# RWKV-7 attention and a dense mixture of experts on one core: chunks of 64 tokens for two batches at a time, with the triangular inverse by substitution on GpSimd

## The chip, the core and the metric

One NeuronCore of a Trainium2 chip. Its engines run side by side, each through its own instructions in order: TensorE (PE; its weight loads are listed apart as PEld) multiplies matrices into PSUM, VectorE (DVE) and ScalarE (ACT) read and write SBUF and PSUM, GpSimd (POOL) works on SBUF, and SyncE (SP) issues DMA transfers. The metric is the device time of one execution in microseconds (us); lower is better. Everything is fp32.

## What is computed

An attention block over 4 batches, 8 heads, 768 tokens and 40 dimensions per head carries a state of 40x40 per head from token to token; its output, with the heads put side by side (3072 tokens x 320), goes through four experts whose outputs are mixed by normalised probabilities.

```python
for t in range(S):                                   # S = 768
    y[:, :, t] = np.einsum('bhd,bhde->bhe', rt, state)
    Sa = np.einsum('bhde,bhe->bhd', state, at)
    state_decay = state * wt[:, :, None, :] - np.einsum('bhd,bhe->bhde', Sa, bt)
    state = state_decay + np.einsum('bhd,bhe->bhde', vt, kt)
...
x = np.ascontiguousarray(attn_out.transpose(0, 2, 1, 3)).reshape(B * S, H * D)
p = domain_probs / (domain_probs.sum(-1, keepdims=True) + 1e-09)
for e in range(E):                                   # E = 4, w1: 320 x 1024, w2: 1024 x 320
    h = np.maximum(x @ w1[e], 0.0)
    out += p[:, e:e + 1] * (h @ w2[e])
```

Both kernels compute the recurrence in chunks: within a chunk, products over pairs of tokens replace the loop, and the rows Sa solve a triangular system (I - F) Sa = A S^T + E V, where F is strictly lower triangular within the chunk.

## The kernel before

A unit is one batch and 128 tokens, which are four chunks of 32; there are 24 units. The 8 heads stand in 4 pairs, one head of each at partitions 0-39 and the other at 64-103; s is that half.

`within(u)` prepares what needs no state. It transposes the inputs so that a head's dimensions are on partitions (`turn`), scans the decays to their running products G (L217) and takes reciprocals (L222), scales A, K and N, and transposes some of them back (`turn_back`). `products` (L204) makes the token-by-token matrices E, C and F; a masked copy keeps the part inside each 32-token chunk. Then comes the inverse of I - F by levels (L264-L281): from blocks of 1 to blocks of 2, 4, 8, 16 and 32, each of four rounds taking a transpose `pq`, a product `pfq` and a product `pqfq` for each half, all of 128x128, with a copy between them. At the end `pu` applies the inverse.

`step(q, c)` runs four times per unit, a chunk each: `psa` gives that chunk's rows of Sa from the state, `psn` turns the state for the outputs, `psd` and two operations of VectorE renew the state. `outputs` makes y (`px`, `py`), scales it and sends it by 8 DMAs, one per head, into xT, the mixture's input, whose rows are the 320 features in groups of 120, 120 and 80.

`mixture` takes 256 tokens (two batches' units): for each expert, products `ph` of all three row groups with 256 columns (L376), a relu by ScalarE (L381), products `po` with 320 columns (L387), and a scaled sum by VectorE (L395). It is a generator; `mix()` runs one of its pieces after each chunk's step and inside the inverse's rounds.

The order of each engine's instructions follows the order of the code, but for a scheduler that may exchange neighbours whose waits would end at other times; on the chip each engine keeps the order that it was given. All names of one PSUM pool share buffers: `big` has three, `small` two, `ph` two and `po` one. SyncE's queue has the loads of the next unit, the writes to xT and the outputs; ScalarE's queue has the weights' loads at the start.

Of the kernel before, what the change touches and what calls it, by code (L numbers as in the profile page):

```python
# [15 lines left out]
def kernel(  # L16
# [34 lines left out]
    L = 32  # L51
    NCK = P // L
    NT = S // P
    NJ = H // 2
    SL = (0, 64)
    NF = F // P
    HG = 3
    NG = -(-H // HG)
    ROWS = [min(HG, H - g * HG) * D for g in range(NG)]
    NTOK = B * S  # L60
    NH2 = 2 * P
    LEVELS = [2 ** i for i in range(L.bit_length() - 1)]

    const = ctx.enter_context(tc.tile_pool(name="const", bufs=1))
    wts = ctx.enter_context(tc.tile_pool(name="wts", bufs=1))
    sb = ctx.enter_context(tc.tile_pool(name="sb", bufs=2))
    mo = ctx.enter_context(tc.tile_pool(name="mo", bufs=2))
    ps = ctx.enter_context(tc.tile_pool(name="ps", bufs=1, space=bass.MemoryType.PSUM))

    def big(name):  # L70
        return ps.tile([P, 512], FP32, name=name, tag="big", bufs=3)

    def small(name, shape):
        return ps.tile(shape, FP32, name=name, tag="small", bufs=2)

    # Constants.
# [7 lines left out]
    def mask(name, half):  # L84
        """1 at [s, t] with s in the left and t in the right half of one block of 2 * half."""
        blk = 2 * half
        f = sb.tile([P, P], FP32, name=name + "_f", tag="Q", bufs=2)
        m = const.tile([P, P], I32, name=name)
        fv = f[:].rearrange("p (n i) -> p n i", i=blk)
        nc.vector.memset(f[:], 1.0)  # L90
        nc.gpsimd.affine_select(
            out=fv, in_=fv, pattern=[[-blk, P // blk], [0, blk]], compare_op=ALU.is_ge, fill=0.0,
            base=0, channel_multiplier=1,
        )
        nc.gpsimd.affine_select(
            out=fv, in_=fv, pattern=[[blk, P // blk], [0, blk]], compare_op=ALU.is_ge, fill=0.0,
            base=half - 1, channel_multiplier=-1,
        )
        nc.vector.memset(fv[:, :, 0:half], 0.0)
        nc.vector.tensor_copy(out=m[:], in_=f[:])  # L100
        return m

    mask_level = [mask(f"mask{h}", h) for h in LEVELS]
    mask_chunk = const.tile([P, P], I32, name="mask_chunk")
    nc.vector.tensor_tensor(out=mask_chunk[:], in0=mask_level[0][:], in1=mask_level[1][:], op=ALU.add)
    for m in mask_level[2:]:
        nc.vector.tensor_tensor(out=mask_chunk[:], in0=mask_chunk[:], in1=m[:], op=ALU.add)
# [309 lines left out]
    while pieces:  # L417
        mix()
# [28 lines left out]
```

## Time and profile before

| what | value |
|---|---|
| time, median of 3 runs | 2876.21 us (2873.59 to 2889.38) |
| profiled execution, first to last instruction | 2906.9 us (its time is recorded as this span alone) |
| TensorE matrix products | 19360 instructions |
| VectorE, ScalarE, GpSimd busy | 753.7, 497.8, 44.2 us |
| mean granted TensorE clock | 0.824 of full speed |
| data moved by DMA | 44.75 MB |

How to read the rows below. The page gives, for each engine, busy time, its share of the span and the number of instructions; a row of digits gives the clock that TensorE was granted in 40 slices of the span, in tenths. The chain of work that ended last goes back from the last instruction to what released it. A group row reads: line, engine, operation, out<-in, shape, count | busy us, mean ns of one | idle time before, and what ended it. A row of the chain in order of time reads: start, us, what. A row of the timeline reads: start, us, engine, line, operation, with merged instructions counted behind an x. A row of the table by windows has the stretch and its length, then busy us and instructions for PE, PEld, DVE, ACT and POOL, then the clock, the share of the DMA engines and GB/s. A mean duration of a TensorE instruction contains its overlap with its neighbours, so the pace is read from rows in which many follow each other.

### The profile page before, as it was taken

The page shows a single profiled execution, that of the slowest core. Times are in us where ns is not written, and L with a number is a line of the kernel's source. Part 1 is how long each engine was busy: PE and PEld are TensorE (multiplying, and loading weights), DVE is VectorE, ACT ScalarE, POOL GpSimd, SP SyncE. Part 2 cuts the span into 40 slices and gives each one's busy share as a digit, 9 for nine tenths or more (in the row PEclk, how much of TensorE's full clock was granted, in tenths as well). Part 3 has the DMA queues.
Part 4 walks back from the last instruction along what each step waited for, and adds up shares of the span by engine and source line. Part 5 has one row for each costly group of instructions (what it writes and reads, how often), then busy time and mean ns, then how long its engine had stood idle before and what let it go on. Part 6 is the DMA issues. An engine that isn't in the chain of part 4 may idle for free.

```text
span 2906.9 us, 43054 instructions
## 1 busy us (share of the span) xinstructions
PE 2781.9 (96%) x19360; PEld 2235.6 (77%) x19360; DVE 753.7 (26%) x1400; ACT 497.8 (17%) x985; POOL 44.2 (2%) x88
## 2 busy tenths in 40 slices
PE   1989999999999999999999999999999999999999
PEld 1778787786887877778778788787777878878867
DVE  2232322123122232222222322222122222322310
ACT  0121121121211211212112121121211212202201
POOL 2000000000000000000000000000000000000000
PEclk9776988887878877968779797796787879969969
DMA  8001001001010010000101101001010010010000
GB/s 172 4 14 17 11 7 21 3 14 22 1 17 13 10 17 6 17 9 9 21 1 16 22 1 17 10 12 17 1 21 5 12 21 3 15 21 1 3 7 5
DMA packets 171710, 44.75 MB, mean 15 GB/s; under 512 B 155400, under 2 KB 170248, under 8 KB 171528
## 3 DMA queue, kind: packets, MB, share of 16 engines
q1 hardware_dynamic: 162816, 31.48, 6.5%
q10 hardware_dynamic: 8712, 10.54, 1.5%
q8 instruction: 152, 2.49, 0.4%
q14 instruction: 30, 0.25, 0.0%
HBM read 34.13 MB, written 3.93 MB: 13 GB/s over the span
## 4 chain that ended last, share of the span: by engine, by line
PE 95%; DMA 2%; DVE 1%; SPq 1%; POOL 0%; issue 0%; ACT 0%; ACTq 0%; DVEq 0%
PE ph L376 21%; PE po L387 19%; PE psd L328 7%; PE pfq L204 6%; PE pqfq L204 6%; PE pq L271 4%; PE psn L316 4%; PE py L352 3%; PE py L348 3%; PE psa L309 3%; PE pf L204 2%; PE pev L250 2%; PE py L349 2%; PE px L204 2%; PE pe L204 2%; PE pc L204 2%
## 5 line engine op out<-in xcount | busy, mean ns | idle before, releaser
L376 PE MATMUL ph<-xT,w_sb 120*128 120x256 f32 (+1 forms) x2304 | 672.8, 431 | 38.8 <-DMA xT<-Y 38.8
L387 PE MATMUL po<-w_sb,hs 128*128 128x320 f32 x1536 | 579.8, 520 | 1.3 <-DVE osb L395 0.6
L376 PEld LDWEIGHTS ph<-xT,w_sb 120*128 120x128 f32 (+1 forms) x2304 | 459.5, 215 | 104.7 <-DMA xT<-Y 21.9
L387 PEld LDWEIGHTS po<-w_sb,hs 128*128 128x128 f32 x1536 | 314.1, 221 | 112.2 <-issue 27.0
L280 DVE COPY_PREDICATED QT<-mask,pqfq 128x512 f32<-128x512 int32 x192 | 140.5, 732 | 560.2 <-PE pqfq L204 560.2
L273 ACT COPY Q<-pq 128x512 f32<-128x512 f32 x192 | 112.5, 586 | 541.7 <-PE pq L271 541.7
L204 PEld LDWEIGHTS pfq<-Q,FT 128*128 128x128 f32 x1536 | 193.6, 199 | 8.1
L204 PE MATMUL pfq<-Q,FT 128*128 128x128 f32 x1536 | 195.9, 282 | 0.0
L328 PEld LDWEIGHTS psd<-natV,KN 32*40 32x40 f32 x1472 | 144.4, 146 | 64.6 <-DVE state L334 42.8
L204 PEld LDWEIGHTS pqfq<-QT,FQ 128*128 128x128 f32 x1536 | 185.2, 191 | 6.6
L381 ACT ACTIVATE hs<-ph 128x512 f32<-128x512 f32 x192 | 114.6, 597 | 432.5 <-PE ph L376 432.5
L204 PE MATMUL pqfq<-QT,FQ 128*128 128x128 f32 x1536 | 188.2, 276 | 0.0
L328 PE MATMUL psd<-natV,KN 32*40 32x40 f32 x1472 | 177.7, 238 | 2.5 <-DVE state L333 2.5
L328 PE MATMUL psd<-Sa,KN 32*40 32x40 f32 x1472 | 176.9, 236 | 0.0
L333 DVE TENSOR_TENSOR state<-psd,state 40x160 f32<-40x160 f32 x184 | 59.3, 322 | 380.5 <-PE psd L328 380.5
L319 ACT COPY SN<-psn 40x160 f32<-40x160 f32 x192 | 54.6, 285 | 590.6 <-PE psn L316 589.1
L328 PEld LDWEIGHTS psd<-Sa,KN 32*40 32x40 f32 x1472 | 148.6, 150 | 2.6
L271 PE MATMUL pq<-ident,QT 128*128 128x128 f32 x768 | 143.1, 316 | 2.5 <-DVE QT L280 1.5
L277 ACT COPY FQ<-pfq 128x512 f32<-128x512 f32 x192 | 112.3, 585 | 151.4 <-PE pfq L204 151.4
L309 PEld LDWEIGHTS psa<-state,AT 40*32 40x32 f32 x1536 | 77.4, 131 | 76.8 <-issue 62.6
L316 PEld LDWEIGHTS psn<-ident,state 40*40 40x40 f32 x1536 | 91.1, 141 | 54.5 <-issue 25.8
L271 PEld LDWEIGHTS pq<-ident,QT 128*128 128x128 f32 x768 | 99.2, 160 | 38.3 <-DVE QT L280 16.4
(103 smaller groups left out, 2527.9 us busy)
## 6 DMA issues: line engine op xcount, KB each, us to landing
w_sb<-in_moe_w_dram ACTq DMA_DIRECT2D x4, 1280.0 KB
w_sb<-in_moe_w_dram ACTq DMA_DIRECT2D x8, 480.0 KB
natR<-in_r_dram SPq DMA_DIRECT2D x24, 160.0 KB
natK<-in_k_dram SPq DMA_DIRECT2D x24, 160.0 KB
natV<-in_v_dram SPq DMA_DIRECT2D x24, 160.0 KB
natW<-in_w_dram SPq DMA_DIRECT2D x24, 160.0 KB
natB<-in_b_dram SPq DMA_DIRECT2D x24, 160.0 KB
natA<-in_a_dram SPq DMA_DIRECT2D x24, 160.0 KB
```

What stands on the lines that cost most here:

```text
L204: nc.tensor.matmul(out=p[:, j * P:(j + 1) * P], lhsT=lhsT[:, j, :], rhs=rhs[:, j, :], start=True, stop=True)
L271: nc.tensor.transpose(out=p[:, j * P:(j + 1) * P], in_=q.QT[s][:, j, :], identity=ident[:])
L273: nc.scalar.copy(out=Q[s][:].rearrange("p j t -> p (j t)"), in_=p[:])
L277: nc.scalar.copy(out=FQ[s][:], in_=products("pfq", FT(2 * u + s), Q[s]))
L280: nc.vector.copy_predicated(out=q.QT[s][:], mask=over_heads(m), data=products("pqfq", FQ[s], q.QT[s]),)
L309: nc.tensor.matmul(out=pa[ck, j, :], lhsT=q.AT[rows(s), j, ck], rhs=st[rows(s), j, :], start=True, stop=True,)
L316: nc.tensor.matmul(out=pn[rows(s), j, :], lhsT=st[rows(s), j, :], rhs=ident[rows(s), rows(s)], start=True, stop=True,)
L328: nc.tensor.matmul(out=pd[rows(s), j, :], lhsT=q.KN[ck, i, h, 0:D], rhs=x[ck, h, 0:D], start=(i == 0), stop=(i == 1),)
L348: nc.tensor.matmul(out=o, lhsT=q.KN[:, 0, h, :], rhs=q.CT[s][:, j, :], start=True, stop=False)
L376: nc.tensor.matmul(out=ph[:, i, :], lhsT=w1_sb[0:ROWS[g], e, g, f * P:(f + 1) * P], rhs=xT[0:ROWS[g], g, :], start=(g == 0), stop=(g == NG ...
L381: nc.scalar.activation(out=hs[:], in_=ph[:], func=ACTF.Relu)
L387: nc.tensor.matmul(out=po[:], lhsT=Hs[f][:, s * P:(s + 1) * P], rhs=w2_sb[:, e, f, :], start=(f == 0), stop=(f == NF - 1),)
```

## The change

The whole attention part is rewritten, and the mixture is cut into smaller pieces.

- A unit is now one chunk of 64 tokens of two batches, the first batch's tokens on partitions 0-63 and the second's on 64-127. There are 24 units as before, and one `step` per unit in place of four. Units are prepared two ahead: the loop runs `step(u)` and `within(u + 2)`.
- The inverse: F's 32x32 diagonal blocks of all heads (4 token groups x 8 heads) are gathered by masked copies into one tile Fd, transposed in 32x32 blocks by VectorE into X, and inverted by column substitution on GpSimd, two instructions for each of 30 columns. VectorE transposes the result into QTc and Qc. One round on TensorE (`pY`, `pQ`, 32x32 products) adds the block beside the diagonal of each 64-token chunk.
- Products over 64 partitions (`products`, `psd`, and the last 64 of the 320 rows of the first weight) go in the order half 0, half 1, half 0, half 1. Products into 64 PSUM partitions (`from_tokens`) alternate the half of the output.
- Scaling is done with tokens on partitions (`pg` turns G back), which saves the transposes back. C K is finished in `within` and added by GpSimd at the end (YC).
- xT's row groups are 128, 128 and 64, the last one kept twice, on both halves. A unit writes 11 DMAs to xT.
- The mixture yields 32 pieces of 256 tokens; the loop takes 16 of them per unit, spread over the 15 places where `step` and `within` yield. PSUM has four `big` buffers and four shared by `ph` and `po`.

The core of the diff, the new side, as the old functions are printed above:

```diff
+    def products(name, lhsT, rhs):
+        p = [big(f"{name}{s}") for s in range(2)]
+        for j in range(NJ):
+            for s in range(2):
+                nc.tensor.matmul(
+                    out=p[s][:, j * P:(j + 1) * P], lhsT=lhsT[half(s), j, :], rhs=rhs[half(s), j, :],
+                    start=True, stop=True,
+                )
+        return [pairs(x[:]) for x in p]
+
+    def from_tokens(name, x, m):
+        p = big(name)
+        for j in range(NJ):
+            for s in range(2):
+                h = 2 * j + s
+                nc.tensor.matmul(
+                    out=p[half(s), j * P:(j + 1) * P], lhsT=x[:, h, :], rhs=m[:, h, :], start=True, stop=True,
+                )
+        return p
...
+        pf = products("pf", q.AT, NT)
+        F10 = sb.tile([P, H, Q], FP32, name="F10")
+        for s in range(2):
+            for i in range(P // Q):
+                o = quarter(i)
+                nc.vector.copy_predicated(
+                    out=fd[o, :, NJ * s:NJ * s + NJ].rearrange("p c j -> p j c"),
+                    mask=mask_low[o, None, :].to_broadcast([Q, NJ, Q]), data=pf[s][o, :, o],
+                )
+            for i in (1, 3):
+                nc.scalar.copy(out=of_slot(F10[quarter(i)], s), in_=pf[s][quarter(i), :, quarter(i - 1)])
+        X = sb.tile([P, Q, Q], FP32, name="X", tag="q", bufs=3)
+        tmp = sb.tile([P, Q * Q // 4], FP32, name="tmp")
+        nc.vector.transpose(out=X[:].rearrange("p c r -> p (c r)"), in_=fd[:].rearrange("p c h -> p (c h)"))
+        for j in range(1, Q - 1):
+            m = Q - 1 - j
+            t = tmp[:, 0:j * m].rearrange("p (c r) -> p c r", c=j)
+            nc.gpsimd.tensor_tensor(
+                out=t, in0=X[:, j:j + 1, j + 1:Q].to_broadcast([P, j, m]),
+                in1=X[:, 0:j, j:j + 1].to_broadcast([P, j, m]), op=ALU.mult,
+            )
+            nc.gpsimd.tensor_tensor(out=X[:, 0:j, j + 1:Q], in0=X[:, 0:j, j + 1:Q], in1=t, op=ALU.add)
+        yield 1
+        KT = turned("KT", q.K)
+        pc = products("pc", VT, q.RT)
+        CT = causal(pc)
+        yield 1
+        pyc = from_tokens("pyc", q.K, CT)
...
+        pe_ = products("pe", KT, q.AT)
+        ET = causal(pe_)
+        yield 1
+        pev = from_tokens("pev", q.V, ET)
...
+        nc.vector.transpose(out=QTc[:].rearrange("p h r -> p r h"), in_=X[:].rearrange("p c r -> p r c"))
+        nc.vector.transpose(out=Qc[:].rearrange("p h c -> p c h"), in_=X[:])
...
+        py = big("pY")
+        for h in range(H):
+            hh = (h % 2) * NJ + h // 2
+            for i in (1, 3):
+                nc.tensor.matmul(
+                    out=py[quarter(i - 1), hh * Q:(hh + 1) * Q], lhsT=F10[quarter(i), h, :],
+                    rhs=QTc[quarter(i), hh, :], start=True, stop=True,
+                )
...
+            for f in range(4):
+                for g in range(2):
+                    nc.tensor.matmul(
+                        out=ph[f % 2][:, f // 2, :], lhsT=w1_sb[:, e, g, (f0 + f) * P:(f0 + f + 1) * P],
+                        rhs=xT[:, g, :], start=(g == 0), stop=False,
+                    )
+                if f % 2:
+                    for i in range(2):
+                        nc.tensor.matmul(
+                            out=ph[i][:, f // 2, :], lhsT=w1_last[i * DT:(i + 1) * DT, e, (f0 + f) // 2, :],
+                            rhs=xT[i * DT:(i + 1) * DT, 2, :], start=False, stop=True,
+                        )
+                    yield 1
...
+    drive(within(units[0]), 0, 1)
+    load(1)
+    drive(within(units[1]), 0, 1)
+    for u in range(NU):
+        q = units[u]
+        if q.bp == 0:
+            xT = sb.tile([P, 3, NTOK], FP32, name="xT", tag="xT", bufs=2)
+        gens = [step(q, xT)]
+        if u + 2 < NU:
+            load(u + 2)
+            gens.append(within(units[u + 2]))
+        drive(chain(*gens), PIECES // 2, 14)
+        if q.bp == B // 2 - 1:
+            work.append(mixture(q.c, xT))
```

The new `step` makes, in this order, `prh` (A times the state; VectorE adds EV), `psn` (the state turned), `prt`, `psa` (the inverse applied), `pst`, `px`, `psd` with the state's renewal, and `py`; between each two of them is a place for a piece of the mixture.

TensorE before, in the middle of the program, where the inverse of a unit begins: `pev` and `pf` end the preparation, then the first round's `pq`, `pfq`, `pqfq` for both halves, with the mixture's `ph` between.

```order
L204 MATMUL pf<-A,N 128x128 x2
L271 MATMUL pq<-ident,QT 128x128 x4
L376 MATMUL ph<-xT,w_sb 128x256 x3
L271 MATMUL pq<-ident,QT 128x128 x4
L376 MATMUL ph<-xT,w_sb 128x256 x2
L204 MATMUL pfq<-Q,FT_134 128x128 x4
L204 MATMUL pfq<-Q,FT_136 128x128 x4
L376 MATMUL ph<-xT,w_sb 128x256 x5
L204 MATMUL pqfq<-QT,FQ 128x128 x8
```

TensorE now, at the end of a unit's preparation in the middle of the program: `pe`, one piece of `ph`, `pev`, nine `po`, then `pY`, which reads QTc, and `pQ`, which reads what ScalarE copied of `pY`.

```order
L216 MATMUL pe_1758<-AT,KT 128x128
L458 MATMUL ph<-xT,w_sb 128x256 x4
L464 MATMUL ph<-xT,w_last 128x256 x2
L228 MATMUL pev<-TT_112,natV_96 64x128 x8
L477 MATMUL po<-w_sb,hs 128x320 x9
L336 MATMUL pY<-QTc,F_1633 32x32 x16
L477 MATMUL po<-w_sb,hs 128x320
L347 MATMUL pQ<-Yq,Qc 32x32
L477 MATMUL po<-w_sb,hs 128x320
L347 MATMUL pQ<-Yq,Qc 32x32 x15
L477 MATMUL po<-w_sb,hs 128x320 x5
```

The twelve products of `pq`, `pfq` and `pqfq` per half and pair are gone, and 16 + 16 small products stand in their place, behind the nine `po`.

GpSimd now, at the end of one unit's substitution and the start of the next one's, with the semaphores that an instruction waits for (Pool is its own engine's; before, this engine had two copies of a constant per unit there):

```order
L296 TENSOR_TENSOR tmp<-X 128x58 [waits Pool_49]
L300 TENSOR_TENSOR X<-X,tmp 128x29x2 [waits Pool_49]
L296 TENSOR_TENSOR tmp<-X 128x30 [waits Pool_49]
L300 TENSOR_TENSOR X<-X,tmp 128x30 [waits Pool_49]
L331 COPY QT_116<-QTc 32x8x32 [waits DVE_49]
L434 TENSOR_TENSOR Y<-Y,YC 128x512 [waits DVE_49,Pool_49]
L296 TENSOR_TENSOR tmp<-X 128x30 [waits DVE_49]
L300 TENSOR_TENSOR X<-X,tmp 128x30 [waits Pool_49]
L296 TENSOR_TENSOR tmp<-X 128x58 [waits Pool_49]
```

And VectorE around the end of the substitution, in the same unit as TensorE's rows above:

```order
L236 COPY_PREDICATED TT_112<-mask_up,pe_1758 128x4x128 [waits PE_49]
L319 STREAM_TRANSPOSE QTc<-X 128x32x32 [waits DVE_49,Pool_49]
L320 STREAM_TRANSPOSE Qc<-X 128x32x32
L487 SCALAR_TENSOR_TENSOR osb<-po,gate,osb 128x320 [waits PE_49] x2
L374 TENSOR_TENSOR RH<-prh,EV 128x512 [waits PE_49]
```

The two transposes wait for GpSimd's last addition; the scaled additions of `po` and the addition to `prh` stand behind them.

More of the change, by code (lines that the diff above doesn't have):

```diff
@@ L220, in within @@
         )
[L221 to L225 removed]
+        q.gl = sb.tile([P, 2 * NJ, 1], FP32, name="gl", tag="gl", bufs=2)
@@ L403 @@
[L403 to L418 removed]
+        nc.vector.tensor_tensor(out=q.K[:, :, 0:D], in0=n["K"][:], in1=gp[:], op=ALU.mult)
@@ new lines, with mix, drive, chain @@
+    PIECES = E * (2 * 2 + 2 * 2)
+    work = []
+    def mix():
+        while work:
+            if next(work[0], None) is not None:
+                return True
+            work.pop(0)
+        return False
+    def drive(gen, n_pieces, n_yields):
+        done = 0
+        for i, _ in enumerate(gen):
+            while done * n_yields < (i + 1) * n_pieces and mix():
+                done += 1
+    def chain(*gens):
+        for g in gens:
+            yield from g
+    drive(within(units[0]), 0, 1)
```

560 lines of the change are left out of this document (286 added, 274 removed).

## The prediction

> **What bounds the kernel now.** I read the page's busy times first, then its chain of work that ended last, the row of the granted clock, and one stretch of the table by windows that leaves out the start and the end.
>
> ```profile
> PE 2781.9 (96%) x19360; PEld 2235.6 (77%) x19360; DVE 753.7 (26%) x1400; ACT 497.8 (17%) x985; POOL 44.2 (2%) x88
> PE 95%; DMA 2%; DVE 1%; SPq 1%; POOL 0%; issue 0%; ACT 0%; ACTq 0%; DVEq 0%
> PEclk9776988887878877968779797796787879969969
> 200.00:2800.00 2600.00, 2554.05 (x17957) 2046.56 (x17955) 686.79 (x1282) 456.91 (x910) 25.75 (x42) 0.82 0.07 12
> ```
>
> TensorE is busy for 2554 of the 2600 us from 200 to 2800 and carries 95% of the chain. GpSimd does nothing there, and the DMA engines are 7% busy. So the time is TensorE's work divided by its clock, whose mean is 0.82 of full speed. The change must be priced in TensorE time and in waits that would put TensorE idle, where it now almost never is.
>
> How fast TensorE goes, shape by shape, I take from rows of the chain of waits at full clock. They tell when one group took over from another, without the overlap of its neighbours:
>
> ```profile
> 303.07 1.79 PE pfq L204 x16
> 312.52 0.44 PE pat L188 x4
> 317.79 0.73 PE psd L328 x16
> 836.31 3.47 PE ph L376 x16
> 2836.93 4.31 PE po L387 x16
> ```
>
> A 128-column instruction costs 0.11 us, a transpose of 128 columns as much, a small one 0.046, `ph` with 256 columns 0.217 and `po` with 320 columns 0.269. Each fp32 product is two such instructions and each transpose one: 768 `pfq` products stand in the page's groups as x1536, 96 `pw` transposes as x96.
>
> **The change, part by part.** Both programs have 24 units of the same 128 rows, so I price one unit and multiply.
>
> Removed first: the inverse by levels, four times per unit.
>
> ```profile
> L204 PE MATMUL pfq<-Q,FT 128*128 128x128 f32 x1536 | 195.9, 282 | 0.0
> L204 PE MATMUL pqfq<-QT,FQ 128*128 128x128 f32 x1536 | 188.2, 276 | 0.0
> L271 PE MATMUL pq<-ident,QT 128*128 128x128 f32 x768 | 143.1, 316 | 2.5 <-DVE QT L280 1.5
> ```
>
> That is 527 us of TensorE time. The four state steps per unit (`psd`, `psa`, `psn`, small products) become one step over 64 tokens of two batches.
>
> New products alternate between partitions 0-63 and 64-127. The old kernel does this once by accident, where the scheduler interleaved `pf` (partitions 0-39) with `pe` (partitions 64-103). This is the timeline of TensorE there:
>
> ```profile
> 605.85 0.82 PE L204 MATMUL pf<-A,N 40*128 40x128 f32 x5
> 606.40 0.37 PE L204 MATMUL pe<-A,K 40*128 40x128 f32 x1
> 606.51 0.27 PE L204 MATMUL pf<-A,N 40*128 40x128 f32 x1
> 606.61 0.27 PE L204 MATMUL pe<-A,K 40*128 40x128 f32 x1
> 606.62 0.27 PE L204 MATMUL pf<-A,N 40*128 40x128 f32 x1
> 606.73 0.27 PE L204 MATMUL pe<-A,K 40*128 40x128 f32 x1
> 606.73 0.27 PE L204 MATMUL pf<-A,N 40*128 40x128 f32 x1
> ```
>
> Two start together, a hundredth of a microsecond or less apart, and the next pair 0.11 us later: such a pair costs one. The price of changing the tile's shape also shows, where `py` alternates 64-column products with 40x40 ones:
>
> ```profile
> 702.37 0.36 PE py L348 x2
> 702.73 0.22 PE py L349 x2
> 702.95 0.42 PE py L352 x8
> ```
>
> The two `py` of L348 that follow the 40x40 group take 0.36, the two behind them 0.22: 0.14 per change, and I use 0.13.
>
> TensorE's work in one new unit at full clock:
> - 44 transposes at 0.11: 4.8 us.
> - 48 products over 64 partitions (`pf`, `pc`, `pe`, `px`, `psd`), in pairs: 96 instructions, 48 slots of 0.11: 5.3.
> - 32 products into 64 PSUM partitions (`pyc`, `pev`, `psa`, `py`): 64 instructions at 0.11: 7.0. No row shows two column halves side by side; it lies between 3.5 (paired) and 11.5 (0.18, as the 0.36 above).
> - 32 products of 64 columns (`prh` and the state's part of `py`): 64 at half of 0.11: 3.5.
> - 32 products of 32x32 (`pY`, `pQ`): 64 at 0.046: 2.9.
> - By the order, 38 changes of tile shape at 0.13: 4.9.
> - The mixture, half of its 256 tokens' work: 64 `ph` at 0.217 make 13.9, the last 64 rows of the first weight in pairs 16 x 0.217 = 3.5, 64 `po` at 0.269 make 17.2: 34.6, in 16 pieces of 2.16.
>
> Sum 63.0 us per unit, 1512 for 24, where TensorE was busy for 2782 us at clock 0.82.
>
> (The Trainium skill, TensorE: Matmul & The Clock Gate, Part 3 on packing small matmuls, says that outputs in separate column groups run side by side too, with 2.38x for three. By it the third item would be 3.5, and the total some 40 us lower; no row here shows it.)
>
> **The new wait.** The inverse of the 32-blocks now runs on GpSimd: 60 instructions in a row, each waiting for the one before, with 30 to 240 elements a partition, 9920 in sum. `pY` on TensorE waits for the end of it, and TensorE is in order. GpSimd's rows of before:
>
> ```profile
> L260 POOL COPY QT<-ident 128x512 f32<-128x512 f32 x48 | 29.4, 614 | 2615.2 <-PE pu L289 2615.2
> L91 POOL TENSOR_SCALAR_AFFINE_SELECT mask_f<-mask_f 128x128 f32<-128x128 f32 x5 | 2.3, 461 | 0.5 <-DVE mask_f L90 0.5
> L79 POOL TENSOR_SCALAR_AFFINE_SELECT ident<-ident 128x128 f32<-128x128 f32 x1 | 0.3, 292 | 0.0
> L433 POOL MEMSET const-float32-0.0<- 128x1 f32 x1 | 0.1, 98 | 0.3 <-issue 0.3
> 1.62 1.20 POOL L91 TENSOR_SCALAR_AFFINE_SELECT mask_f<-mask_f 128x128 f32<-128x128 f32 x2
> ```
>
> Fixed cost 0.098 us; a copy costs (614-98)/512 = 1.0 ns an element. No instruction with two inputs stands in the trace. Lower end: the copy's rate, 9.9 + 60 x 0.098 = 16 us. Upper end: the first masks, in runs of 2 and 4 elements, took about 0.6 us for 128 elements, so 4.7 ns each and 47 us in all. I take twice the copy, because two inputs must be read: 19.8 + 5.9, and for short runs (0.6 - 0.292)/64 = 4.8 ns for each of the 930 runs, 4.5. That is 30 us.
>
> (The Trainium skill, GPSIMD Engine Reference, section 3.1, gives 4497 ns for a two-input add of 2048 elements, 2.2 ns each, and calls this engine the wrong one for elementwise work. By it the elements take 22 us and the same sum 32; the trace has no such row.)
>
> Around it stand VectorE's pieces, from these rows:
>
> ```profile
> L333 DVE TENSOR_TENSOR state<-psd,state 40x160 f32<-40x160 f32 x184 | 59.3, 322 | 380.5 <-PE psd L328 380.5
> L217 DVE TENSOR_TENSOR_SCAN G<-w_shift,first 128x528 f32<-128x528 f32 x24 | 30.2, 1257 | 25.6 <-ACT w_shift L215 25.6
> L247 DVE COPY_PREDICATED ET<-mask_chunk,pe 128x512 f32<-128x512 int32 x48 | 34.6, 721 | 111.8 <-PE pe L204 111.8
> L222 DVE RECIPROCAL GI<-G 128x512 f32<-128x512 f32 x24 | 80.2, 3343 | 0.1
> ```
>
> Eight masked copies of 128 elements at 0.3 (nearest, the 160-element row) make 2.4; two block transposes of 1024 elements, between the masked copy's and the scan's 1.4 and 2.4 ns an element less their fixed part, I put at 1.2 each; 0.2 for the hand-overs. From the end of `pf` to `pY`: 2.4 + 1.2 + 30 + 1.2 + 0.2 = **35 us**, 21 to 52 by the ends.
>
> What covers it: in the order, 5.25 mixture pieces (11.3), `pKT`, `pc`, `pyc`, `pe`, `pev` (5.7) and 13 changes of shape (1.7), 18.7 us at full clock, about 21.5 at 0.87. So TensorE idles some 13 us per unit, and nothing overtakes `pY`. On VectorE the two block transposes wait at the head for the same end; behind them stand two scaled additions of `po` and the addition of `prh`, which TensorE needs only behind `pY`. On GpSimd the copies into QT and the addition of YC follow; they are used a stage later.
>
> From `pY` to the next `pf` TensorE has 63.0 - 18.7 = 44.3 us of work. I take clock 0.87 there (0.82 before; dense pieces stand between all stages now, but a long idle time comes first): 51 us, with 2 us for hand-overs that one piece of 2.16 us doesn't cover (the reciprocal of 320 elements, 3343 x 320/512 = 2.1, is the longest): **53**. A unit's turn is 35 + 53 = 88 us.
>
> The loads become 12 DMAs of half the size per unit and the writes to xT 11 in place of 8, on a queue whose engines are 7% busy; each has a unit's turn to land. I cost them at nothing; without that cover it would be some microseconds a unit.
>
> Start and end:
>
> ```profile
> 51.94 1.12 PE L188 MATMUL pb<-ident,natB 128*128 128x128 f32 x4 [17.27 <-ACT w_shift L215]
> 2820.00:2907.00 87.00, 81.06 (x320) 62.53 (x320) 4.41 (x8) 9.55 (x16) 0.00 (x0) 0.94 0.02 6
> ```
>
> The weights hold ScalarE's queue until about 52 us, as before. Then come four units' preparations without a mixture, their chains wholly bare: 44 + 46 + 2 x 58 (with a step of 12) = 206, so 258. Twenty turns of 88 make 1760. Two last steps take 30 each, and 50 pieces at 2.16 and full clock 108, with the output 170. Sum 258 + 1760 + 170 = 2188 us against the span of 2906.9. The median of the runs is 2876.21, 0.9894 of that span, so 2165 us.
>
> **The rivals.**
> - *The substitution is hidden*: GpSimd goes at the copy's rate, 16 us. The chain is 21 us, as long as its cover, and TensorE stays the bound: 63/0.87 + 3 = 75 per turn, start 202: 202 + 1508 + 170 = 1880, or 1860 us. For it speaks that GpSimd's rows are all short; against it, that each instruction reads two operands and waits for the last.
> - *The clock stays down behind the idle time*: with 0.7 between `pY` and `pf` the turn is 35 + 66 = 101 and the sum 258 + 2020 + 180 = 2458, or 2432 us. The clock row shows 0.7 in many slices of a TensorE that never idles.
> - *The substitution takes the bound, and the kernel is slower*: the sum is 1348 + 24 x chain, equal to 2907 at a chain of 65 us, GpSimd at 1.0 us an instruction. At 1.3 us (78 us, chain 83) it is 3340, or 3305 us. The first masks' 0.6 us for 128 elements is the dearest row; this needs twice that, so I give it little.
>
> **How the numbers follow.** Forecast 0.58, hidden 0.23, low clock 0.13, slower 0.05, and 0.01 for a balance near nothing. The likeliest gives 2165 us, on its own 2030 to 2300. The range takes in the hidden case and the low clock: 1820 to 2430. Faster by over 0.5% (about what a measurement of this kernel can tell from no change) has 0.94, the same 0.01, slower 0.05.
>
> **What would show it.** GpSimd's `tmp` and `X` groups, 60 per unit, near 0.5 us each; `pY` first in TensorE's waits, released through VectorE's `QTc` by GpSimd, near 13 us a unit; TensorE's busy share near 80%; paired starts in `pf`, `px`, `psd` and the `w_last` products; clock 0.8 to 0.9. A GpSimd mean under 0.3 or over 0.9 us makes the chain wrong; no idle time at `pY` with a time over 2000 makes TensorE's own sum wrong.

## The result, and the profile after

| | before | after |
|---|---|---|
| median of the runs side by side | 2882.15 us (2873.59 to 2889.38, 4 runs) | 2210.34 us (2209.20 to 2211.01, 4 runs) |
| ratio | | 0.7666 (95%: 0.7642 to 0.7690) |
| profiled span | 2906.9 us | 2209.1 us |
| mean granted TensorE clock | 0.824 | 0.833 |

The forecast was 2165 us with a range of 1820 to 2430. From the page of the changed kernel: busy times, the row of the clock, the chain that ended last, the groups that matter, and then two rows of the waits of TensorE and VectorE (engine and line, what was waited for: us in all, times, longest).

```profile
PE 1522.0 (69%) x11592; PEld 1115.2 (50%) x11592; DVE 636.7 (29%) x930; ACT 318.3 (14%) x667; POOL 803.4 (36%) x1596
...
PEclk9656777977978979879788798797797887978999
...
PE 48%; POOL 34%; DVE 11%; issue 5%; DMA 1%; ACT 0%; SPq 0%; ACTq 0%; DVEq 0%; POOLq 0%
...
L296 POOL TENSOR_TENSOR tmp<-X 128x30 f32<-128x30 f32 (+4 forms) x720 | 348.1, 483 | 545.4 <-DVE X L292 490.9
...
L300 POOL TENSOR_TENSOR X<-X,tmp 128x30 f32<-128x30 f32 (+4 forms) x720 | 369.6, 513 | 56.4
...
L319 DVE STREAM_TRANSPOSE QTc<-X 128x1024 f32<-128x1024 f32 x24 | 47.6, 1983 | 686.4 <-POOL X L300 686.4
L283 DVE COPY_PREDICATED Fd<-mask_low,pf 32x128 f32<-32x128 int32 x192 | 139.0, 724 | 115.1 <-PE pf L216 112.4
```

```profile
PE pY L336 <- DVE QTc L319: 577.3, 24, 31.1
DVE QTc L319 <- POOL X L300: 686.4, 24, 30.2
```

TensorE is no longer the bound: it is busy for 69% of the span, and GpSimd and VectorE carry 45% of the chain that ended last. Most of TensorE's idle time sits in one wait. Of 687 us (2209.1 - 1522.0) it stood 577.3 at `pY`, 24 us a unit, for VectorE's transposition QTc, and VectorE stood there for GpSimd's last addition to X. This is one such unit, in the timeline of TensorE (start, us, what, and in brackets the idle time ahead):

```profile
1024.12 1.06 PE L216 MATMUL pf<-NT,AT 64*128 64x128 f32 x16
...
1039.58 5.11 PE L477 MATMUL po<-w_sb,hs 128*128 128x320 f32 x18
1069.23 1.07 PE L336 MATMUL pY<-QTc,F 32*32 32x32 f32 x32 [24.54 <-DVE QTc L319]
...
1079.82 1.20 PE L369 MATMUL prh<-AT,state 128*64 128x64 f32 x32
1080.94 1.09 PE L205 MATMUL psn<-ident,state 128*128 128x128 f32 x8
...
1089.83 1.09 PE L228 MATMUL psa<-QT,RHt 128*64 128x128 f32 x16
1090.86 1.99 PE L458 MATMUL ph<-xT,w_sb 128*128 128x256 f32 x8
...
1101.78 0.44 PE L420 MATMUL py<-TT,n_tok 128*64 128x128 f32 x4
...
1103.73 2.42 PE L477 MATMUL po<-w_sb,hs 128*128 128x320 f32 x8
```

In the same unit on VectorE, and GpSimd's first two and last of the 60 instructions:

```profile
1025.21 5.91 DVE L283 COPY_PREDICATED Fd<-mask_low,pf 32x128 f32<-32x128 int32 x8 [3.57 <-PE pf L216]
1031.22 1.25 DVE L292 STREAM_TRANSPOSE X<-Fd 128x1024 f32<-128x1024 f32 x1
...
1067.11 1.97 DVE L319 STREAM_TRANSPOSE QTc<-X 128x1024 f32<-128x1024 f32 x1 [29.67 <-POOL X L300]
```

```profile
1032.54 0.24 POOL L296 TENSOR_TENSOR tmp<-X 128x30 f32<-128x30 f32 x1 [19.90 <-DVE X L292]
1032.86 0.24 POOL L300 TENSOR_TENSOR X<-X,tmp 128x30 f32<-128x30 f32 x1
...
1066.81 0.27 POOL L300 TENSOR_TENSOR X<-X,tmp 128x30 f32<-128x30 f32 x1
```

`pf` ends at 1025.18 and `pY` starts at 1069.23: a chain of 44.0 us from one to the other, and it takes 44.0 to 44.6 us in the other units too. Of it 5.9 are the masked copies, 1.25 and 1.97 the two transpositions, and 34.6 GpSimd. Its instructions are busy for 29.9 us a unit, (348.1 + 369.6)/24; the rest is 0.08 us between each two that depend on each other, as between 1032.54 + 0.24 and 1032.86.

### The profile page after: what moved, and what is told of

Its sections match the earlier page's. It is cut to its first block, busy times and chain, and to the rows that moved or that the text cites. A ratio compares the mean times of both kernels' runs of the same rounds, so it can differ in the third digit from the quotient of the medians.

```text
span 2209.1 us, 28307 instructions
## 1 busy us (share of the span) xinstructions
PE 1522.0 (69%) x11592; PEld 1115.2 (50%) x11592; DVE 636.7 (29%) x930; ACT 318.3 (14%) x667; POOL 803.4 (36%) x1596
## 4 chain that ended last, share of the span: by engine, by line
PE 48%; POOL 34%; DVE 11%; issue 5%; DMA 1%; ACT 0%; SPq 0%; ACTq 0%; DVEq 0%; POOLq 0%
POOL X L300 17%; POOL tmp L296 16%; PE po L477 16%; PE ph L458 11%; DVE Fd L283 6%; PE ph L464 4%; DVE QTc L319 2%; PE psd L402 2%; PE prh L369 1%; PE psn L205 1%; DVE X L292 1%; PE px L216 1%; PE pf L216 1%; PE pQ L347 1%; PE psa L228 1%
## 5 line engine op out<-in xcount | busy, mean ns | idle before, releaser
L296 POOL TENSOR_TENSOR tmp<-X 128x30 f32<-128x30 f32 (+4 forms) x720 | 348.1, 483 | 545.4 <-DVE X L292 490.9
L477 PE MATMUL po<-w_sb,hs 128*128 128x320 f32 x1536 | 489.6, 468 | 0.0
L336 PE MATMUL pY<-QTc,F 32*32 32x32 f32 x768 | 25.5, 236 | 577.3 <-DVE QTc L319 577.3
L458 PE MATMUL ph<-xT,w_sb 128*128 128x256 f32 x1536 | 390.6, 395 | 2.9 <-DMA xT<-Y 2.9
L300 POOL TENSOR_TENSOR X<-X,tmp 128x30 f32<-128x30 f32 (+4 forms) x720 | 369.6, 513 | 56.4
L458 PEld LDWEIGHTS ph<-xT,w_sb 128*128 128x128 f32 x1536 | 277.6, 192 | 69.1 <-issue 29.3
L319 DVE STREAM_TRANSPOSE QTc<-X 128x1024 f32<-128x1024 f32 x24 | 47.6, 1983 | 686.4 <-POOL X L300 686.4
L283 DVE COPY_PREDICATED Fd<-mask_low,pf 32x128 f32<-32x128 int32 x192 | 139.0, 724 | 115.1 <-PE pf L216 112.4
L464 PE MATMUL ph<-xT,w_last 64*128 64x256 f32 x768 | 148.2, 436 | 0.0
L464 PEld LDWEIGHTS ph<-xT,w_last 64*128 64x128 f32 x768 | 63.2, 188 | 69.1 <-issue 67.7
L259 DVE RECIPROCAL gp<-gp 128x320 f32<-128x320 f32 x24 | 51.4, 2143 | 0.0
```

Source lines behind the costliest of these rows:

```text
L259: nc.vector.reciprocal(out=gp[:], in_=gp[:])
L283: nc.vector.copy_predicated(out=fd[o, :, NJ * s:NJ * s + NJ].rearrange("p c j -> p j c"), mask=mask_low[o, None, :].to_broadcast([Q, NJ, Q ...
L296: nc.gpsimd.tensor_tensor(out=t, in0=X[:, j:j + 1, j + 1:Q].to_broadcast([P, j, m]), in1=X[:, 0:j, j:j + 1].to_broadcast([P, j, m]), op=AL ...
L300: nc.gpsimd.tensor_tensor(out=X[:, 0:j, j + 1:Q], in0=X[:, 0:j, j + 1:Q], in1=t, op=ALU.add)
L319: nc.vector.transpose(out=QTc[:].rearrange("p h r -> p r h"), in_=X[:].rearrange("p c r -> p r c"))
L336: nc.tensor.matmul(out=py[quarter(i - 1), hh * Q:(hh + 1) * Q], lhsT=F10[quarter(i), h, :], rhs=QTc[quarter(i), hh, :], start=True, stop=True,
```

## The experiments

**Is the chain the bound, or does the idle time bring the clock down?** Two kernels shorten the substitution, the first to every second column, the second to none. Their inverses are therefore not the right ones; each ran once.

```diff
-        for j in range(1, Q - 1):
+        for j in range(1, Q - 1, 2):       # e1_half
+        for j in range(0):                 # e2_none
```

> Every second column of the substitution is left out (30 GpSimd instructions per unit in place of 60), so the inverse is not the reference's. Chain theory (pf to pY, 44 us, stands on the path of all 24 units, and TensorE idles 21 to 25 us at its end): the chain is cut by some 17 us, less than the idle time, so all of it counts: 2210 - 24 x 17 = about 1800 us, idle time at pY about 6 us a unit. Rival (the clock gives it back: TensorE without idle time is granted 0.82 as in the old kernel): a turn of 63/0.82 + 3 = 80 us, about 2010 us. Second rival (something else of the turn is nearly as late, VectorE's or ScalarE's part): 2100 us or more.

> The substitution is left out whole (no GpSimd instruction between X and QTc), so the inverse is not the reference's. Chain theory: the cut of 34.6 us is more than the idle time of 23 us, so the time falls to TensorE's own work, a turn of 65 us: 2210 - 24 x 23 = about 1660 us, no idle time at pY, and the second half of the substitution is worth only 6 x 24 = 140 us more than the first half's 410. Rival (clock): about 2010 us as with half of it.

Measured: 1855.6 us with half, 1622.3 us without. The waits at `pY` with half, and the row of the clock without:

```profile
PE pY L336 <- DVE QTc L319: 271.3, 24, 13.8
```

```profile
PEclk9677999999999999999999999999999999999999
```

The chain falls from 44.0 to 26.8 us, the wait from 577 to 271, and without the substitution there is none. The clock goes up as the idle time goes, from 0.833 to 0.907 and 0.947. So the wait is the bound and the clock follows it, not the other way round. With half, the time is 55 us above the 1800 expected. The wait fell by 12.8 us a unit where the chain fell by 17.2, because the order of TensorE changed with the edit: in the middle of the program one to three pieces of the mixture fewer stand between `pf` and `pY`.

**Is it GpSimd's pace?** The same substitution runs on VectorE, in one run.

```diff
-            nc.gpsimd.tensor_tensor(
+            nc.vector.tensor_tensor(
                 out=t, in0=X[:, j:j + 1, j + 1:Q].to_broadcast([P, j, m]),
...
-            nc.gpsimd.tensor_tensor(out=X[:, 0:j, j + 1:Q], in0=X[:, 0:j, j + 1:Q], in1=t, op=ALU.add)
+            nc.vector.tensor_tensor(out=X[:, 0:j, j + 1:Q], in0=X[:, 0:j, j + 1:Q], in1=t, op=ALU.add)
```

> The 60 instructions of the substitution run on VectorE in place of GpSimd; the result is the same. Chain theory: an instruction of 160 elements takes VectorE 0.32 us, so 60 take 19 to 23 us in place of 34.6, with some 3 us of other VectorE work between them: the chain is 10 us shorter, about 1970 us. Rival (VectorE's queue becomes the late one: the masks and the state's renewal stand behind the substitution): 2100 us or more, with TensorE waiting at px, pyc or prh.

Measured: 1777.8 us, far below both. Its group row and its waits:

```profile
L300 DVE TENSOR_TENSOR X<-X,tmp 128x30 f32<-128x30 f32 (+4 forms) x720 | 237.8, 330 | 22.6
```

```profile
PE pY L336 <- DVE QTc L319: 108.9, 24, 21.9
```

An instruction takes 330 ns where GpSimd took 513, and the chain falls to 34.5 us. That alone would leave some 14 us of idle time. But the order changed as well: three to four more pieces of the mixture now stand ahead of `pY`, and the wait at `pY` in the middle of the program is about 2 us a unit. The expectation missed because it held TensorE's order fixed. The 1778 us are thus VectorE's pace and a better cover together; the run doesn't part them.

**Must the wait be there at all?** X isn't needed before the state step of its own unit, a whole turn later. Everything behind the substitution (QTc, Qc, `pY`, `pQ`, the copies to QT) becomes a function of its own, which runs behind the step of the unit before; X gets a buffer to itself.

```diff
+        q.X, q.F10 = X, F10
+    def tail(q):
+        X, F10 = q.X, q.F10
         Qc = sb.tile([P, Q, Q], FP32, name="Qc", tag="q", bufs=2)
...
         gens = [step(q, xT)]
+        if u + 1 < NU:
+            gens.append(tail(units[u + 1]))
```

> The work behind the substitution (the two block transposes, pY, pQ and the copies into QT) of unit u+2 is moved from the end of its preparation to the next turn, behind the step of unit u+1, so that the step's 30 us of TensorE work stand between pf and pY too. All is computed as the reference does. Chain theory: the cover is 50 us against a chain of 44, the idle time goes, and the time is TensorE's own work: about 1660 us, ratio to the old kernel 0.58. Rival (clock): about 2010 us. Second rival (the chain is only moved: another wait, for QT at psa or for SN's buffer, takes its place): 2100 us or more.

Measured: 1835.2 us (1834.7 to 1837.6), ratio to the kernel before 0.6305 (0.6255 to 0.6354). `pY` no longer waits in the middle of the program; another place does. From the waits of TensorE and the timelines of VectorE and TensorE:

```profile
PE py L424 <- DVE TT L236: 127.6, 21, 12.7
```

```profile
968.14 2.01 DVE L323 STREAM_TRANSPOSE QTc<-X 128x1024 f32<-128x1024 f32 x1 [24.94 <-POOL X L300]
970.06 1.28 DVE L236 COPY_PREDICATED TT<-mask_up,px 128x512 f32<-128x512 int32 x2
```

```profile
970.78 1.09 PE L424 MATMUL py<-TT,n_tok 128*64 128x128 f32 x3 [8.99 <-DVE TT L236]
```

In the order, QTc stands ahead of the masked copies of `px` on VectorE, though the code has it behind. So it waits at the head of VectorE for GpSimd until 968, and the copies that `py` needs, whose `px` is long done, stand behind it. The wait at `pY` became a wait at `py`, by way of the second engine's order.

So the next kernel ties the two transpositions to a place: a copy of one element, which the transposition overwrites, makes QTc stand behind the scaling of K in the following unit's preparation, and the call of `tail` moves there.

```diff
+        if after is not None:
+            nc.vector.tensor_copy(out=QTc[:, 0, 0:1], in_=after.K[:, 0, 0:1])
         nc.vector.transpose(out=QTc[:].rearrange("p h r -> p r h"), in_=X[:].rearrange("p c r -> p r c"))
...
+            gens.append(behind(within(units[u + 2]), 2, tail(units[u + 1], units[u + 2])))
```

> As in the run that moved the use of the inverse one unit later, but VectorE's two transpositions of X are tied (by a copy of one element into QTc, which the transposition overwrites) behind the scaling of K in the following unit's preparation, so that they cannot stand ahead of the state step's masked copies. X is ready 44 us after the end of pf, the scaling of K comes some 56 us after it. If the wait on GpSimd is all that stood between 1835 us and TensorE's own work, no wait above 1 us per unit is left at py or pY, the turn falls from 71 to about 65 us, as with the substitution left out, and the time is 1640 us (1615 to 1680). If VectorE's or PSUM's order only moves the wait again, it stays at 1750 to 1840 us, and the waits name the new place.

Measured: 1678.9 us (1676.9 to 1683.4), ratio 0.5791 (0.5755 to 0.5826). VectorE's timeline at that place, then TensorE's waits:

```profile
1151.59 0.15 DVE L324 COPY QTc<-k_tok 128x1 f32<-128x1 f32 x1
1151.66 1.95 DVE L326 STREAM_TRANSPOSE Qc<-X 128x1024 f32<-128x1024 f32 x1
1153.46 1.91 DVE L325 STREAM_TRANSPOSE QTc<-X 128x1024 f32<-128x1024 f32 x1
```

```profile
PE pY L342 <- DVE QTc L325: 77.1, 22, 29.6
PE pyc L228 <- DVE TT L236: 50.1, 24, 3.9
```

The transpositions start with no wait in front. Of the 77.1 us at `pY`, 47.6 belong to the first two units, which have nothing to hide them (29.6 and 18.0); the others are about 1.5 us each. GpSimd is as slow as ever (810 us busy), and it costs next to nothing.

**The masked copies.** One takes 724 ns for 32x128 elements, as much as the 721 for 128x512 (TT<-px). Fd is laid out so that a copy writes 32 neighbouring elements a row in place of elements 128 bytes apart.

```diff
-    nc.vector.tensor_copy(out=fd[:], in_=diagf[:, :, None].to_broadcast([P, Q, Q]))
+    nc.vector.tensor_copy(out=fd[:], in_=diagf[:, None, :].to_broadcast([P, Q, Q]))
...
-                    out=fd[o, :, NJ * s:NJ * s + NJ].rearrange("p c j -> p j c"),
+                    out=fd[o, NJ * s:NJ * s + NJ, :],
...
-        nc.vector.transpose(out=X[:].rearrange("p c r -> p (c r)"), in_=fd[:].rearrange("p c h -> p (c h)"))
+        nc.vector.transpose(out=X[:], in_=fd[:].rearrange("p h c -> p c h"))
```

> The gathering tile Fd is laid out so that each masked copy writes 32 neighbouring elements a row instead of elements 128 bytes apart; the transposition of it then reads with a stride. Nothing else changes. If the written stride makes the masked copies dear (0.724 us each, as much as the masked copy of 512 elements, 0.721), they fall to about 0.3, eight of them from 5.9 to 2.4 us, and the transposition goes from 1.25 to about 1.97, as the strided QTc takes: the chain from the end of pf to pY falls from 44.0 to 41.3 us and the time by 24 x 2.8, to about 2145 us. If the cost sits in the PSUM side or in the mask, the copies stay at 0.72 and the time is 2210 to 2230 us.

Measured: 2147.7 us (2147.1 to 2151.8), and the groups:

```profile
L283 DVE COPY_PREDICATED Fd<-mask_low,pf 32x128 f32<-32x128 int32 x192 | 57.0, 297 | 118.0 <-PE pf L216 115.3
L292 DVE STREAM_TRANSPOSE X<-Fd 128x1024 f32<-128x1024 f32 x24 | 47.1, 1961 | 1.3
```

The stride was the cost: 297 ns in place of 724, while the transposition that now reads with the stride pays 0.7 us. The chain is 41.2 us, and 2.8 us a unit are worth 62.6 us, near the 67 of 24 chains.

Both edits together, the tied transpositions and the layout of Fd, as their diffs stand above:

> The version with the tied transpositions, and Fd with its masked copies' rows side by side. The chain on GpSimd is off the path there, so the 2.8 us that the layout takes off it are worth nothing by themselves. But pyc waits 50.1 us in 24 times for the masked copies TT, which stand on VectorE behind the eight copies into Fd (5.9 us, now 2.4): if that is the wait, it goes and the time falls by some 40 to 50 us, to about 1635 us (1620 to 1650). If VectorE is not what pyc waits for in truth, the time stays at 1670 to 1685 us.

Measured: **1618.6 us** (1613.3 to 1623.9), ratio 0.5653 (0.5609 to 0.5697), the fastest of the study and 27% below the changed kernel. TensorE's waits, and the starts of `pf` two units apart:

```profile
PE pyc L228 <- DVE TT L236: 11.8, 14, 0.9
```

```profile
1055.84 0.93 PE L216 MATMUL pf<-NT,AT 64*128 64x128 f32 x11
...
1175.49 1.16 PE L216 MATMUL pf<-NT,AT 64*128 64x128 f32 x16
```

The copies are off the path to `pY` here, yet they stood ahead of the masked copies for `pyc`; that wait went from 50.1 to 11.8 us. The time fell by 60 us, more than the 40 to 50 expected; this wait is 38 of them, and where the rest lies is not shown. A turn, from one unit's `pf` to the next one's, is (1175.49 - 1055.84)/2 = 59.8 us on average here: TensorE's own work, with 1.9 us of idle time in it, 1.4 of that at `pY`.

**What the pairs are worth.** On the version with the tied transpositions, where TensorE is the bound, three kernels take pairs away: of row halves (`pf`, `pc`, `pe`, `px`, `psd`), of column halves (`pyc`, `pev`, `psa`), and of the mixture's last 64 rows.

```diff
-        for j in range(NJ):
-            for s in range(2):
+        for s in range(2):                 # e11_halves: products, psd
+            for j in range(NJ):            # e12_columns: from_tokens
...
-                            out=ph[i][:, f // 2, :], lhsT=w1_last[i * DT:(i + 1) * DT, e, (f0 + f) // 2, :],
-                            rhs=xT[i * DT:(i + 1) * DT, 2, :], start=False, stop=True,
+                            out=ph[i][:, f // 2, :], lhsT=w1_last[0:DT, e, (f0 + f) // 2, :],
+                            rhs=xT[0:DT, 2, :], start=False, stop=True,      # e13_onehalf
```

> The version with the tied transpositions, with the products over 64 partitions (pf, pc, pe, px, psd) in the order half 0 four times, half 1 four times, so that neighbours share their rows. If pairs of halves cost one slot, as the prediction took it, 96 instructions a unit take 96 slots of 0.11 us in place of 48: 5.3 us more a unit, 127 us, 1806 us in all; if the clock falls besides, since fewer rows work at a time, up to 1900 us. If the order of halves makes no difference, 1680 us.

> The version with the tied transpositions, with the products into 64 PSUM partitions (pyc, pev, psa) in the order half 0 four times, half 1 four times; py keeps its order. If the halves of the output run in pairs, 48 instructions a unit take 48 slots of 0.11 us in place of 24: 2.6 us more a unit, 63 us, 1742 us in all. If they never ran in pairs, as the prediction's middle value of 7.0 us had it, 1680 us.

> The version with the tied transpositions, with the last 64 rows of the first weight taken twice from partitions 0 to 63, never from 64 to 127: half of the hidden features then get another feature's last 64 rows, so a part of the mixture's result is another one; instructions and sizes are as before. If such pairs cost one slot, 32 instructions of 256 columns a unit take 32 slots of 0.217 us in place of 16: 3.5 us more a unit, 83 us, 1762 us in all. If only the change of shape counts and not the pair, 1680 us.

Measured against 1678.9: row halves apart 1768.5 (+90), column halves apart 1701.1 (+22), the last rows on one half 1746.7 (+68). One row each from TensorE's timelines, first the three with pairs, then each without, from its own kernel (row halves, column halves, last rows):

```profile
1128.02 1.09 PE L228 MATMUL psa<-QT,RHt 128*64 128x128 f32 x16
...
1139.55 0.70 PE L470 MATMUL ph<-xT,w_last 64*128 64x256 f32 x4
...
1163.87 1.06 PE L216 MATMUL pf<-NT,AT 64*128 64x128 f32 x16
```

```profile
1155.01 1.71 PE L216 MATMUL pf<-NT,AT 64*128 64x128 f32 x16
```

```profile
1134.24 1.58 PE L228 MATMUL psa<-QT,RHt 128*64 128x128 f32 x16
```

```profile
1157.10 1.13 PE L470 MATMUL ph<-xT,w_last 64*128 64x256 f32 x4
```

All three kinds of pairs run side by side. Each was worth less than the expectation said (127, 63 and 83 us). For sixteen instructions it took 16 x 0.11 = 1.76 us without pairs and 0.88 with them, a gain of 0.88. The rows, whose last instruction runs over into what follows, differ by 0.65 (`pf`) and 0.49 (`psa`): in the trace's records the first instructions of the second half still start beside the last ones of the first half. (The Trainium skill, TensorE: Matmul & The Clock Gate, Part 3 on packing small matmuls, has column groups side by side; the 1.09 us of 16 `psa`, against 1.58, agree.)

**What the levels were worth before.** Two kernels on the old side leave the four rounds of the inverse out. The first leaves out the mixture's calls between them as well, the second keeps them.

```diff
-        for m in mask_level[1:]:
+        for m in []:                       # e9_nolevels
...
         for m in mask_level[1:]:           # e14_pieces: nothing but the two calls is left
+            mix()
+            mix()
```

> The kernel before with the four rounds of the inverse by levels left out (its inverse is then only the first level's, and the mixture's pieces that ran inside the rounds run later). The prediction priced these rounds at 527 us of TensorE time by their rows. If they cost that at the granted clock of 0.82, the time falls by about 640 us to 2240 us. If they cost their slots alone at full clock (72 us per thousand... 3840 instructions at 0.11 = 422 us) it falls to about 2400 us. If waits between the short stages that are left turn up, it stays above 2450 us.

> The kernel before with the four rounds of the inverse by levels left out, but with the mixture's pieces called at the same places, eight per unit there. The run that left out both took 2599 us in place of the 2240 that the rounds' 527 us of TensorE time at clock 0.82 would give, at a granted clock of 0.72. If the clock fell because the pieces of the mixture stood elsewhere, this one takes about 2250 us at 0.82. If it fell because the 128x128 products of the rounds are gone and the small products of the state's steps make up more of the work, it stays at 2500 to 2620 us with a clock of 0.70 to 0.75.

Measured: 2598.6 us (2572 and 2625) and 2319.1 us (2290 to 2326), where the kernel before took 2899 and 2897. The middle of the three programs by windows (stretch; busy us of PE, PEld, DVE, ACT, POOL; clock; DMA share; GB/s), in the order before, without calls, with calls:

```profile
200.00:2000.00 1800.00, 1766.39 (x12451) 1416.03 (x12449) 475.00 (x893) 312.82 (x623) 18.39 (x30) 0.82 0.07 12
```

```profile
200.00:2000.00 1800.00, 1772.77 (x11255) 1379.07 (x11255) 450.40 (x888) 191.31 (x427) 22.18 (x36) 0.70 0.08 14
```

```profile
200.00:1800.00 1600.00, 1567.25 (x11267) 1229.04 (x11266) 440.56 (x866) 199.64 (x435) 20.96 (x34) 0.86 0.09 15
```

With the calls kept, the levels are worth 578 us, near the 527 us that their rows show in the kernel before. The 640 of the first expectation counted the clock twice: 3840 instructions at 0.11 are 422 us at full clock and 515 at 0.82, so the busy time of 527 us already holds the clock. The other kernel has the same 15520 products in another order, TensorE 98% busy all the same, and takes 280 us more at a clock of 0.70. The time lies where the expectation put waits between the short stages, but there are none; it is the clock, and with the pieces at their places the clock is back. (The profiled executions are the longer of each, 2625 and 2326 us; the shortest of each lie as far apart, 2572 and 2290.)

## Why the prediction was right

The time came 2% above the forecast, in the case that it called likeliest, and the mechanism was the one forecast: the bound moved to the chain through GpSimd, and TensorE waits for it at `pY`. That the time came so near is partly luck, since two errors of 9 us cancel in the turn. Of the signs named, TensorE's busy share missed: 69% where 80% was forecast, as the idle time is nearly twice the forecast.

| per unit, us | predicted | measured (mean) |
|---|---|---|
| eight masked copies into Fd | 2.4 | 5.9 |
| transpositions X and QTc | 1.2 + 1.2 | 1.25 + 1.97 |
| GpSimd, 60 instructions | 30 | 34.6 (29.9 busy) |
| chain, end of `pf` to `pY` | 35 | 44.0 |
| TensorE idle at `pY` | 13 | 24 |
| `pY` to the next end of `pf` | 53 | 44 (49 to 50 and 38 to 39 by turns) |
| turn | 88 | 88 (93 to 94 and 82 to 83 by turns) |

The unit shown above begins one of the longer turns; why they alternate is not shown. The idle time at `pY` is 11 us longer than forecast: 9 from the chain, and 2 because the work that covers it took 19.5 us (1025.18 to 1044.69, at a granted clock of 1.00) where the prediction had 21.5 at 0.87.

**The bound moves to the chain on GpSimd**: this was right. Half of the substitution, or none, shows it by time and by wait.

**GpSimd's price**: the sum for the instructions was right (30 against 29.9), but this too is luck in part. These are the dearest and the cheapest of the additions:

```profile
L300 POOL TENSOR_TENSOR X<-X,tmp 128x240 f32<-128x240 f32 x48 | 32.2, 671 | 3.8
L300 POOL TENSOR_TENSOR X<-X,tmp 128x30 f32<-128x30 f32 x48 | 12.1, 252 | 3.8
```

An element of them costs (671 - 252)/210 = 2.0 ns, as taken from twice the copy's rate. What is left of the 252 ns is a fixed part of 0.19 us, where the sum had 0.098; that is some 5.5 us more in 60 instructions. The 4.5 us for short runs are hardly there: the first addition to X, one run of 30 elements, takes 0.24 us, and the last, 30 runs of one, 0.27. What the sum lacked altogether was the 0.08 us from one dependent instruction to the next, 4.7 us in all; the step "0.2 for the hand-overs" counted those around the 60 and none between them. (By the Trainium skill, GPSIMD Engine Reference, section 3.1, the sum was 32; its 2.2 ns an element is a little above the 2.0 of the rows here. Its rule that elementwise work goes to VectorE holds for the pace, 513 against 330 ns, but not for the time: once nothing waits for GpSimd, the kernel with it takes 1619 us.)

**The masked copies**: they were mis-sized, 0.3 us each where they took 0.724. The nearest row by elements (160) had no mask and wrote side by side. With the layout changed, 0.3 is what they take, so the step that failed is that the written stride was left out of account.

**The rest of the turn**: this was mis-sized the other way. The windows of the changed kernel are, behind a `pY`, the next 42 us and then two parts of the same turn; those of the fastest version are its middle and the two turns above:

```profile
1070.00:1112.00 42.00, 42.00 (x323) 29.84 (x320) 12.21 (x22) 7.89 (x16) 2.07 (x3) 0.88 0.04 8
1069.23:1079.23 10.00, 10.00 (x78) 6.23 (x78) 1.98 (x2) 1.45 (x4) 1.50 (x4) 0.50 0.01 2
1080.00:1119.30 39.30, 39.30 (x313) 29.31 (x311) 12.04 (x22) 8.49 (x16) 1.27 (x1) 1.00 0.10 19
```

```profile
600.00:1400.00 800.00, 775.16 (x6499) 573.08 (x6496) 324.67 (x530) 172.86 (x366) 443.74 (x868) 0.99 0.12 23
1055.84:1175.49 119.65, 115.76 (x985) 85.87 (x984) 49.28 (x80) 26.44 (x56) 66.49 (x130) 1.00 0.13 24
```

The mean clock was right, 0.88 for the 0.87 assumed, but it is a mean of two speeds. In this trace the granted clock is 0.50 or 1.00 and nothing between. Here it is 1.00 until TensorE has stood idle for 4.5 us, then 0.50 until 10.7 us after `pY` has begun, and 1.00 again. So a wait costs more than its idle time: behind the 24 waits at `pY` TensorE works 7 to 14 us each at half clock, 217 us in all, of which 109 are lost.

TensorE's work was too high: the sum of 63.0 us a unit at full clock stands against 115.76/2 = 57.9 in the two turns of the fastest version at clock 1.00. The rows of the unit shown above say where: `prh` takes 1.12 us for the 1.76 it was priced at, `psa` 1.03 for 1.76, `py` with its changes of shape 1.95 (from 1101.78 to 1103.73) for 4.4, and `pY`, even at half clock, 1.00 for 1.5. All four write to parts of PSUM's partitions in turn. That such products run side by side is shown for `psa` by the kernel with the column halves apart; `prh` and `py` have no such kernel, but in the trace's records two of them start within 0.01 us and the next two some 0.06 to 0.11 us later. For `pY` it is only read off its row. The 2 us for hand-overs were not there either: TensorE is busy for 42.00 of the 42 us.

**Start, turns and end**: the first `pY` starts at 90.0 us where the sum had 96, and the next three follow after 58, 71 and 74 us where it had 46, 58 and 58. The longer chain is 9 us of each step; what the rest is stays open. So the fourth `pY` (unit 3) starts at 293.4 against 258. Twenty turns take 1748.5 us, up to the last `pY` at 2041.9, against 1760, and the end 167 against 170. That makes 2209 against 2188. The factor from the span to the median, 0.9894 before, is 1.0006 after; it made half of the miss of 45 us.

**What was costed at nothing**: for the loads and writes by DMA this was right; DMA is 1% of the chain that ended last. On VectorE nothing that mattered waited behind QTc, as was said; in the kernel with the transpositions moved, something did.

**The rivals**: the hidden substitution did not happen by GpSimd's pace, but the moved transpositions make it happen by order, and its price there (1860 us) was too high, because it kept a clock of 0.87 and a work of 63.0 for a TensorE that never waits; they are 0.99 and 57.9. The low clock of 0.7 behind the idle time did not come; the mean was 0.88. (That rival's own sum is rounded up: 44.3/0.7 + 2 is 65.3 and not 66, so its time would be some 14 us less.) The slower case needed a GpSimd instruction of 1.3 us; it takes 0.50.

So the change gave 672 us in the runs side by side. The fastest version, whose TensorE works through the same 11592 products without most of the wait, gave 1279 (2898 to 1619); so the change gave back some 590 us. By the two pages TensorE's idle time falls from 687 to 189 us, of it the wait at `pY` from 577.3 to 82.1, and its busy time from 1522.0 to 1427.6 us with the same number of products. So of the 590 some 500 are idle time and 94 are slower work, near the 109 lost at half clock behind the waits.

## What to carry to other kernels

A slow engine costs nothing until something waits for it in order. Look for the first use of its result and move that use by a whole turn, before making the engine faster. Then look at the engine in between, whose order may put the waiting instruction ahead of work that others need, and tie it to a place. Price a wait of TensorE at more than its idle time, since here half clock followed each one. Where a sum comes out right, measure its terms too: here two errors of 9 us a unit cancelled, and only the wait itself said that 590 us were still to be had.

## What the runs showed of the hardware that was not expected

- The granted clock can depend on how the same TensorE work is ordered: 0.70 against 0.86 in the middle of two programs with the same 15520 products and TensorE 98% busy in both, worth 280 us. What in the order decides it was not tried out. (The Trainium skill, TensorE: Matmul & The Clock Gate, Part 1, lets the gate go by how busy TensorE was shortly before; busy by the profile isn't enough to tell here.)
- The clock rises with fewer waits: its mean is 0.833 after, 0.907 with half the substitution and 0.947 with none. In the changed kernel TensorE works 7 to 14 us behind each wait at `pY` before it is granted full clock again.
- A masked copy that writes 4-byte elements 128 bytes apart takes 724 ns for 128 elements a row, and 297 side by side; a block transposition of 1024 elements takes 1.25 us with both sides in order, and 1.9 to 2.0 with one or both read or written across.
